# Chunk 1's first channel product as seven half-size products, with a newly searched job order

## The chip, the cores and the metric

The kernel runs on one core of a Trainium2 chip. The core has TensorE (PE in the profile; its weight loads are PEld), VectorE (DVE), ScalarE (ACT), GpSimd (POOL) and SyncE (SP, which here only issues DMAs). TensorE writes its results into eight banks of PSUM, from which VectorE and ScalarE read them. The metric is the time of one execution in microseconds, taken as the median of several runs. A profile is one execution of its own.

## The reference

Two layers follow each other. Shapes: q, k, v are (8 batches, 8 heads, 576 tokens, 64), omega is (128, 64).

```python
def phi(x):                                   # x already scaled by 64 ** -0.25
    h = x @ omega.T - sum(x * x) / 2
    return exp(h - max(h)) / sqrt(128)
q_p, k_p = phi(q), phi(k)
kv  = k_p^T @ v                               # per batch and head, 128 x 64
z   = sum(k_p over tokens)
x   = (q_p @ kv) / (q_p @ z + 1e-6)           # (8, 576, 512) after joining heads

h   = relu(x^T @ w_tok1) @ w_tok2             # over tokens: 576 -> 256 -> 576
u   = x + h^T
out = u + relu(u @ w_ch1) @ w_ch2             # over channels: 512 -> 1536 -> 512
```

The result is float32; the kernel works in float16 with float32 sums in PSUM.

## The kernel before

**Stages.** For each batch b (0 to 7): attention (`attention`), the token mix (`token_mix`, or `token_mix_first` for batch 0), then the channel mix (`channel_mix`) of "chunk" c = b, which covers the batch's first 512 tokens. The last 64 tokens of all batches are gathered and make chunk 8. Of batches 2 to 7, q and k go through DRAM: GpSimd issues DMAs that cast them to float16 into scratch (`load_transposed`, lines 407 to 418), and SP issues DMA transposes that bring them back (line 428, tiles qT and kT). The token mix ends in u, which SP turns with another DMA transpose into uT (line 852), the operand of the channel mix. The first attention jobs of a batch (lines 599 and 707 for k, 669 and 719 for q) read kT and qT.

**Channel mix, two forms.** The first product is u (512 tokens x 512) by w_ch1 (512 x 1536). In the plain form (lines 1178, 1184, 1186) it is 12 jobs, one for each 128 hidden columns: four matmuls of 512 columns into one bank, then one relu by ScalarE or VectorE (line 338 or 340) into tile r3. In the fast form (`channel_in_fast`, matmuls at line 1107) both operands are cut into halves, 2 x 2 blocks, and the four block products are made out of seven, in Winograd's way. It works on three groups of hidden columns (m = 0, 1, 2), each with seven products of four 256-column matmuls into the banks X, Y and Z. It needs four sums of blocks of uT (line 343 through `tt`), eight sums of blocks of w_ch1 (`weight_sums`, made once and kept in one buffer of the qT ring, one of the kT ring and a small tile), three copies per group that keep a bank for later (line 334, into parts of r3, qp and kp buffers), three joins per group (line 1131, VectorE adds a kept copy to a bank) and relus over the joined blocks. The second product has its own seven-product form (`channel_out_fast`, line 989), used by chunks 1 to 8; its sums (tile S) are of 768 columns, and chunk 0 uses the plain form (line 1212).

Which form the first product takes is one number:

```python
if c >= FAST_IN:
    channel_out_fast(c, key, channel_in_fast(c, key, jt))
    return
```

and the sums of the weights are added to the program ahead of that chunk (`if b == FAST_IN: weight_sums(b - 1.0)`).

**The order.** The program builds a list of jobs (1528 of them before), each with its engine, what it depends on and which buffers it takes and gives back. It does not choose their order while building: `ORDER` is a written list of job numbers, found by a search beforehand (negative numbers are filler matmuls that keep TensorE busy in the head, line 1252), `SLOT` says which buffer of a ring each taker gets, and `MOVED` puts single jobs on another engine than their usual one. Each engine works through its own jobs strictly in that order, so a job that waits holds all the jobs of its engine behind it. This goes for SP too, whose queue holds loads back, u transposes and stores in one line, and for GpSimd, which issues the casting DMAs between its sums. Jobs marked `port=True` on VectorE and GpSimd also wait for each other in turn (`turns`).

Of the kernel before, what the change touches and what calls it, by code (L numbers as in the profile page):

```python
# [213 lines left out]
def kernel(  # L214
# [28 lines left out]
    RT = ST // 2  # L243
    RA = R + RT
    NPE = 2
    FAST_IN = 2
    SPLIT = ()
    HALVES = ()
    RW = S * 4 // P
# [1036 lines left out]
```

## Time and profile before

| What | Value |
|---|---|
| Median of 3 runs | 268.33 us (268.24 to 268.38) |
| Profiled execution | 270.67 us |
| Its span, first to last instruction | 268.9 us |
| Granted TensorE clock, mean | 0.998 |
| PE busy | 257.9 us, 96% |
| DVE busy | 231.7 us, 86% |
| ACT busy | 183.0 us, 68% |
| POOL busy | 158.9 us, 59% |

A busy share is an average over the whole span. TensorE's matmuls are pipelined: the mean duration of one (273 ns for 256 columns) is longer than the pitch at which they follow each other, so the cost of a stream is read from the length of an unbroken stretch divided by its count. In a timeline, what stands in brackets at the end of a row is the time that the engine stood idle before it and what ended that.

### The profile page before, as it was taken

Reading aid. Unit: us, or ns where it says so; the run is one execution under the profiler, and the core shown is the slowest. Engines: PE = TensorE matmul, PEld = TensorE weight load, DVE = VectorE, ACT = ScalarE, POOL = GpSimd, SP = SyncE. Lnnn points to the kernel's source line nnn. Section 1 sums busy time; section 2 is a strip of 40 time slices with the busy share of each in tenths; the row PEclk is TensorE's granted clock in tenths of the full one; section 3 lists DMA queues with packets and bytes.
Section 4 is the critical chain, followed back from the end, with each engine's and each line's share of the span. In section 5 each row is a group of like instructions: output and inputs, shape, how many; then the busy total and the mean of one; then the engine's idle time right before and its main releaser. Section 6 shows DMA issues by size and latency. Waiting matters only on the chain.

```text
span 268.9 us, 6989 instructions
## 1 busy us (share of the span) xinstructions
PE 257.9 (96%) x2752; PEld 190.6 (71%) x2752; DVE 231.7 (86%) x494; ACT 183.0 (68%) x425; POOL 158.9 (59%) x160
## 2 busy tenths in 40 slices
PE   4999999999999999989999999999999999999993
PEld 2568455454667985768768777897696788888882
DVE  3999978599999998889999999998987898788982
ACT  1997982089885896879988989878865482273400
POOL 8765553061897966987498852745775004927171
PEclk9999999999999999999999999999999999999999
DMA  7999999999999999999999927844350513040144
GB/s 192 199 208 200 205 207 184 175 220 186 240 168 143 175 207 187 121 198 210 175 222 189 240 85 80 119 85 95 105 152 0 80 67 112 0 157 4 41 146 127
DMA packets 81826, 39.72 MB, mean 148 GB/s; under 512 B 64033, under 2 KB 77729, under 8 KB 81601
## 3 DMA queue, kind: packets, MB, share of 16 engines
q0 software_dynamic: 31712, 17.61, 44.7%
q1 hardware_dynamic: 48560, 19.50, 34.7%
q10 hardware_dynamic: 1520, 2.16, 2.3%
q8 instruction: 21, 0.34, 0.5%
q14 instruction: 13, 0.10, 0.1%
HBM read 35.95 MB, written 16.52 MB: 195 GB/s over the span
## 4 chain that ended last, share of the span: by engine, by line
PE 81%; DMA 7%; POOL 6%; issue 2%; DVE 2%; ACT 1%; POOLq 0%
PE bank L989 23%; PE bank L1107 21%; PE bank L1178 7%; PE bank L1212 4%; PE bank L831 4%; PE bank L844 4%; DMA k<-in_k_dram 4%; DMA uT<-u 3%; PE bank L707 3%; PE bank L796 3%; PE bank L763 2%; PE bank L719 2%; POOL S L343 2%; POOL vs L343 1%; POOL uT L343 1%
## 5 line engine op out<-in xcount | busy, mean ns | idle before, releaser
L562 ACT ACTIVATE kp<-bank 128x512 f16<-128x512 f32 x64 | 35.8, 610 | 13.5 <-PE bank L707 13.1
L338 ACT ACTIVATE r<-bank 128x512 f16<-128x512 f32 (+1 forms) x50 | 29.1, 606 | 20.1 <-PE bank L1107 9.9
L989 PEld LDWEIGHTS <-r 128*128 128x128 f16 x384 | 36.9, 98 | 6.8 <-issue 1.0
L562 ACT ACTIVATE qp<-bank 128x512 f16<-128x512 f32 x64 | 36.7, 631 | 2.5 <-PE bank L719 2.4
L740 DVE TENSOR_REDUCE km<-kp 128x8 f16<-128x1024 f16 x32 | 38.1, 1205 | 0.5 <-ACT kp L562 0.5
L343 POOL TENSOR_TENSOR vs<-v,vs 128x512 f16<-128x512 f16 x22 | 23.7, 1082 | 16.0 <-DVE vs L744 5.5
L1107 PE MATMUL bank<-uT,wc 128*128 128x256 f16 x228 | 30.5, 273 | 1.2 <-DMA uT<-u 1.2
L989 PEld LDWEIGHTS <-S 128*128 128x128 f16 x288 | 27.6, 98 | 4.4 <-POOL S L343 0.2
L1107 PEld LDWEIGHTS <-wc 128*128 128x128 f16 x252 | 23.5, 98 | 5.7 <-DMA uT<-u 1.7
L343 POOL TENSOR_TENSOR S<-r,S 128x768 f16<-128x768 f16 x15 | 24.4, 1641 | 4.5 <-DVE vbd L644 3.4
L989 PE MATMUL bank<-T,r 128*128 128x256 f16 x192 | 23.8, 273 | 0.1
L989 PE MATMUL bank<-T,S 128*128 128x256 f16 x192 | 23.6, 273 | 0.0
L989 PE MATMUL bank<-wc,r 128*128 128x256 f16 x192 | 23.4, 273 | 0.0
L812 ACT ACTIVATE x<-bank,rc 128x64 f16<-128x64 f32 x100 | 22.4, 348 | 0.4 <-DVE rc L803 0.4
L343 POOL TENSOR_TENSOR uT<-uT,uT 128x512 f16<-128x512 f16 x10 | 11.6, 1158 | 17.9 <-PE bank L1107 15.8
L338 ACT ACTIVATE r<-r 128x512 f16<-128x512 f16 (+1 forms) x21 | 16.7, 822 | 7.5 <-DVE r L1131 7.5
L1107 PE MATMUL bank<-uT,qT 128*128 128x256 f16 x126 | 21.7, 272 | 0.0
L847 DVE TENSOR_TENSOR u<-x,bank 128x512 f16<-128x512 f16 x28 | 17.8, 680 | 4.3 <-PE bank L844 4.2
L1107 PE MATMUL bank<-uT,kT 128*128 128x256 f16 x126 | 21.4, 273 | 0.0
L1178 PE MATMUL bank<-uT,wc 128*128 128x512 f16 x88 | 20.5, 380 | 0.0
L969 DVE TENSOR_TENSOR o<-u,bank 128x512 f32<-128x512 f16 x28 | 19.0, 677 | 1.8 <-PE bank L989 1.7
L814 DVE TENSOR_TENSOR x<-bank,rc 128x320 f16<-128x320 f32 x44 | 20.0, 477 | 0.4
(158 smaller groups left out, 612.5 us busy)
## 6 DMA issues: line engine op xcount, KB each, us to landing
out_dram<-o SPq DMA_DIRECT2D x11, 512.0 KB, 4.5
q<-in_q_dram POOLq DMA_DIRECT2D x6, 576.0 KB, 9.2
wc<-in_moe_w_ch_dram POOLq DMA_DIRECT2D x4, 768.0 KB, 13.1
k<-in_k_dram POOLq DMA_DIRECT2D x6, 512.0 KB, 9.4
v<-in_v_dram POOLq DMA_DIRECT2D x6, 512.0 KB, 8.9
out_dram<-o SPq DMA_DIRECT2D x6, 256.0 KB, 3.3
r<-in_q_dram POOLq DMA_DIRECT2D x4, 288.0 KB, 7.6
v<-in_v_dram POOLq DMA_DIRECT2D x4, 256.0 KB, 10.8
```

What stands on the lines that cost most here:

```text
L338: nc.scalar.activation(out=out, in_=in_, func=AF.Relu)
L343: (nc.gpsimd if eng == "POOL" else nc.vector).tensor_tensor(**kw)
L562: nc.scalar.activation(out=out, in_=in_, func=AF.Exp, bias=0.0, scale=1.0)
L740: nc.vector.reduce_max(out=t_km[place("km", (b, hp))], in_=src_, axis=AX.X)
L812: nc.scalar.activation(out=to[:, j], in_=ps[:, j], func=AF.Copy, scale=rc[:, j : j + 1])
L814: nc.vector.tensor_tensor(out=to, in0=ps, in1=rc.unsqueeze(2).broadcast_to((P, NJ + 1, D)), op=ALU.mult)
L831: nc.tensor.matmul(ps, w1m[:, j, tb * P : (tb + 1) * P], x[:, j, :], start=False, stop=(j == NJ - 1))
L847: nc.vector.tensor_tensor(out=t_u[place("u", b)][:, j, :], in0=t_x[place("x", b)][:, j, :], in1=bank(n), op=ALU.add)
L969: nc.vector.tensor_tensor(out=o, in0=a, in1=ps, op=ALU.add)
L989: nc.tensor.matmul(ps[:, j * DH : (j + 1) * DH], a[:, cb, j * P : (j + 1) * P], w[:, cb, :], start=(bank_of(b, j0) not in held and j == j0 ...
L1107: nc.tensor.matmul(ps[:, n, :], w(a)[:, (2 * m + n) * P : (2 * m + n + 1) * P], x_[:, a], start=(what in ("P1", "P2", "P5") and n == 0 and ...
L1178: nc.tensor.matmul(ps, wc1[:, db, cb * P : (cb + 1) * P], moving(db), start=(db == 0), stop=(db == ND - 1))
```

## The change

`FAST_IN` goes from 2 to 1, so chunk 1's first channel product takes the fast form: 12 jobs of four 512-column matmuls are replaced by 21 of four 256-column matmuls, with the block sums, kept copies, joins and relus that belong to them. The sums of the weights are added ahead of chunk 1 and not ahead of chunk 2, with the same eight operations. The list has 1556 jobs. `ORDER`, `SLOT` and `MOVED` are replaced as a whole: the part that loads and transposes batch 0 and works on its attention keeps the order that it has on each engine (but for one filler), and what follows comes from a new search, in which a DMA transpose that is issued late holds the Sync engine. Nothing else of the program differs.

```diff
 ORDER = [
-    2, 38, 16, 3, 7, 6, 4, 9, 12, 10, 0, -8, 41, 1, 14, 39, 42, 40, 47, 48, 8, 11, 13, 21, 22, 19, 17, 5, 78, 49,
...
-    1507, 1520, 1521, 1508, 1509, 1523, 1522, 1516, 1510, 1511, 1525, 1517, 1524,
+    2, 3, 7, 6, 5, 4, 9, 12, 10, 38, 16, 0, 8, 1, -8, 41, 14, 11, 39, 47, 42, 13, 40, 78, 21, 48, 49, 79, 22, 50,
...
+    1545, 1534, 1544, 1535, 1548, 1549,
 ]
 SLOT = (
...
 MOVED = {
...
-    164: "DVE", 167: "DVE", 175: "ACT", 181: "DVE", 185: "DVE", 201: "ACT", 206: "ACT", 208: "DVE", 246: "ACT",
...
+    164: "DVE", 171: "DVE", 173: "DVE", 175: "ACT", 177: "DVE", 181: "DVE", 183: "ACT", 191: "ACT", 196: "ACT",
+    201: "ACT", 202: "ACT", 208: "DVE", 227: "DVE", 244: "DVE", 246: "ACT", 249: "ACT", 261: "DVE", 263: "DVE",
+    278: "DVE", 283: "ACT", 291: "DVE", 303: "POOL", 304: "POOL", 307: "POOL", 308: "POOL", 310: "POOL",
...
 }
@@
     NPE = 2
-    FAST_IN = 2
+    FAST_IN = 1
     SPLIT = ()
```

More of the change, by code (lines that the diff above doesn't have):

```diff
@@ L22 @@
 ORDER = [
[74 rows of a table removed]
[76 rows of a table added]
 ]
 SLOT = (
-    "0001203405067101232540760102330123012460751230021432701142623113003145101237261500434567001253621417"
-    "2150621753341006702115023246105163020133704015231042211507121124306303205126456737421201062402061324"
-    "2201113074125061353027113542131203072261135000431170621452237061221304432567571103611241001041715030"
-    "6221337501163231215013020260321073200100010703124612013205143605627400120546347304507210610110320157"
-    "1420300721233501471320035233112200011221320521731023116120117130614372100420310271260020516724301023"
-    "6725230000411213015637023061102723600532000126030203101200276053120076215110320241567642470362100006"
-    "3007332211237261213236102101614301200111415623037214100571321651720100310110630265310623321775354117"
-    "6203003031213052672420310456017132120231212603105207101053126027754356120701052010202101302113105263"
-    "41010712315012156720400712050333201120117050423160"
+    "0000123405067100112325407601024336027512403012021134270113326230041301512726135100453467002524611337"
+    "5140163100743215074060101212405330202627104331240221317311402157012426315240475667327104061702021200"
+    "4601731201412765022103012301114226315001232220764110521311314200050310001124725610051747415012000376"
+    "1522014751320012301624017511573020643200110120206240320512310576312045123250674102041306354722011113"
+    "2065421720030643700521331020113621050421716021011632312500034262012322670411317603361300542766427173"
+    "5140015163327201031056301410020117361212102413607122031205617320013231406105312467276342113000126710"
+    "3251410023211351042112254323215413031211225076143201150217300453622104510010260023150103306612061347"
+    "0423106351033610241215700614210152312017026502430070532647223005610746537047250171202035223520331320"
+    "065172001243113040352114740312600140312013200165071340"
 )
@@ L111 @@
     103: "DVE", 111: "ACT", 120: "DVE", 137: "DVE", 142: "ACT", 149: "DVE", 151: "DVE", 155: "DVE", 161: "ACT",
-    164: "DVE", 167: "DVE", 175: "ACT", 181: "DVE", 185: "DVE", 201: "ACT", 206: "ACT", 208: "DVE", 246: "ACT",
-    261: "DVE", 269: "ACT", 278: "DVE", 280: "DVE", 291: "DVE", 312: "DVE", 318: "DVE", 324: "DVE", 328: "POOL",
-    330: "POOL", 332: "POOL", 334: "POOL", 349: "ACT", 394: "DVE", 396: "DVE", 402: "ACT", 411: "DVE", 413: "DVE",
-    428: "DVE", 430: "DVE", 433: "ACT", 452: "POOL", 453: "POOL", 455: "POOL", 459: "POOL", 460: "POOL", 478: "ACT",
@@ L116 @@
-    509: "ACT", 510: "ACT", 514: "POOL", 516: "POOL", 517: "POOL", 518: "POOL", 586: "ACT", 595: "DVE", 603: "ACT",
-    617: "ACT", 637: "POOL", 638: "POOL", 639: "POOL", 640: "POOL", 656: "ACT", 690: "POOL", 692: "POOL",
-    694: "POOL", 696: "POOL", 744: "ACT", 778: "ACT", 781: "ACT", 798: "ACT", 813: "POOL", 814: "POOL", 815: "POOL",
-    816: "POOL", 831: "ACT", 832: "ACT", 866: "POOL", 868: "POOL", 869: "POOL", 870: "POOL", 920: "ACT", 940: "ACT",
-    971: "ACT", 992: "POOL", 994: "POOL", 1009: "ACT", 1025: "ACT", 1026: "ACT", 1041: "ACT", 1043: "POOL",
@@ L121 @@
-    1044: "POOL", 1046: "POOL", 1050: "POOL", 1066: "ACT", 1101: "ACT", 1112: "DVE", 1152: "ACT", 1167: "POOL",
-    1168: "POOL", 1169: "POOL", 1170: "POOL", 1174: "DVE", 1185: "ACT", 1186: "ACT", 1202: "ACT", 1217: "ACT",
-    1220: "POOL", 1222: "POOL", 1224: "POOL", 1226: "POOL", 1271: "DVE", 1277: "ACT", 1291: "ACT", 1325: "ACT",
-    1333: "DVE", 1348: "POOL", 1355: "DVE", 1362: "DVE", 1363: "ACT", 1373: "DVE", 1380: "ACT", 1387: "DVE",
-    1395: "ACT", 1396: "ACT", 1397: "POOL", 1398: "POOL", 1400: "POOL", 1404: "POOL", 1426: "POOL", 1427: "POOL",
@@ L126 @@
-    1429: "POOL", 1445: "ACT", 1449: "DVE", 1461: "ACT", 1477: "ACT", 1480: "POOL", 1481: "POOL", 1485: "POOL",
-    1514: "ACT", 1516: "POOL", 1517: "POOL", 1518: "ACT", 1519: "SP", 1520: "ACT", 1521: "SP", 1524: "ACT",
-    1525: "SP",
+    164: "DVE", 171: "DVE", 173: "DVE", 175: "ACT", 177: "DVE", 181: "DVE", 183: "ACT", 191: "ACT", 196: "ACT",
+    201: "ACT", 202: "ACT", 208: "DVE", 227: "DVE", 244: "DVE", 246: "ACT", 249: "ACT", 261: "DVE", 263: "DVE",
+    278: "DVE", 283: "ACT", 291: "DVE", 303: "POOL", 304: "POOL", 307: "POOL", 308: "POOL", 310: "POOL",
@@ new lines @@
+    312: "POOL", 313: "POOL", 314: "POOL", 346: "ACT", 366: "POOL", 368: "POOL", 369: "POOL", 370: "POOL",
+    418: "ACT", 430: "DVE", 472: "ACT", 487: "POOL", 505: "ACT", 506: "ACT", 538: "ACT", 540: "POOL", 542: "POOL",
+    544: "POOL", 546: "POOL", 597: "ACT", 625: "DVE", 628: "ACT", 648: "ACT", 665: "POOL", 666: "POOL", 667: "POOL",
+    668: "POOL", 684: "ACT", 699: "ACT", 716: "ACT", 718: "POOL", 720: "POOL", 724: "POOL", 772: "ACT", 806: "ACT",
+    841: "POOL", 842: "POOL", 843: "POOL", 844: "POOL", 859: "ACT", 876: "ACT", 894: "POOL", 896: "POOL",
@@ new lines @@
+    897: "POOL", 900: "POOL", 979: "DVE", 982: "ACT", 985: "ACT", 1002: "ACT", 1020: "POOL", 1021: "POOL",
+    1037: "ACT", 1053: "ACT", 1054: "ACT", 1069: "ACT", 1070: "ACT", 1074: "POOL", 1077: "POOL", 1078: "POOL",
+    1093: "ACT", 1094: "ACT", 1129: "ACT", 1146: "ACT", 1160: "ACT", 1174: "DVE", 1195: "POOL", 1196: "POOL",
+    1197: "POOL", 1198: "POOL", 1202: "DVE", 1207: "DVE", 1212: "DVE", 1214: "ACT", 1229: "ACT", 1230: "ACT",
+    1234: "DVE", 1246: "ACT", 1248: "POOL", 1249: "POOL", 1252: "POOL", 1254: "POOL", 1269: "ACT", 1270: "ACT",
@@ L129 @@
+    1297: "DVE", 1299: "DVE", 1305: "ACT", 1336: "ACT", 1339: "ACT", 1373: "POOL", 1376: "POOL", 1406: "DVE",
+    1408: "ACT", 1423: "ACT", 1426: "POOL", 1427: "POOL", 1428: "POOL", 1431: "POOL", 1432: "POOL", 1448: "ACT",
+    1449: "ACT", 1455: "POOL", 1461: "DVE", 1466: "DVE", 1472: "ACT", 1488: "ACT", 1496: "DVE", 1505: "ACT",
+    1508: "POOL", 1509: "POOL", 1542: "ACT", 1544: "POOL", 1545: "POOL", 1550: "ACT", 1551: "SP",
 }
```

146 rows, old and new, of the table ORDER are left out of this document.

## The prediction

> **What bounds the kernel now.** I read the page's first part, then a table of engine time by stage, then the chain of waits, then the timelines round the two places where TensorE stands still. In the table the columns behind the window's length are the busy us of PE, weight loads, VectorE, ScalarE and GpSimd, each with its count.
>
> ```profile
> span 268.9 us, 6989 instructions
> PE 257.9 (96%) x2752; PEld 190.6 (71%) x2752; DVE 231.7 (86%) x494; ACT 183.0 (68%) x425; POOL 158.9 (59%) x160
> ...
> 0.00:10.00 10.00, 5.63 (x48) 4.15 (x50) 4.78 (x15) 4.12 (x7) 7.82 (x17) 1.00 0.89 192
> 10.00:20.00 10.00, 9.63 (x183) 5.48 (x178) 9.95 (x24) 10.00 (x27) 7.58 (x11) 1.00 1.21 208
> ...
> 60.00:70.00 10.00, 10.00 (x86) 5.02 (x85) 8.97 (x21) 9.37 (x19) 3.44 (x4) 1.00 0.99 195
> 70.00:80.00 10.00, 10.00 (x106) 5.90 (x103) 9.54 (x26) 8.22 (x23) 9.98 (x11) 1.00 1.15 203
> 80.00:90.00 10.00, 10.00 (x117) 8.01 (x115) 9.72 (x18) 6.75 (x15) 8.28 (x7) 1.00 1.22 141
> 90.00:100.00 10.00, 10.00 (x137) 9.13 (x134) 9.46 (x27) 9.30 (x29) 8.37 (x11) 1.00 1.10 206
> 100.00:110.00 10.00, 9.30 (x86) 5.61 (x84) 8.18 (x18) 6.80 (x14) 6.71 (x8) 1.00 1.46 182
> 110.00:120.00 10.00, 8.67 (x109) 6.94 (x109) 8.72 (x16) 8.41 (x23) 8.81 (x8) 1.00 1.07 141
> ```
>
> The 11.0 us without a matmul (268.9 - 257.9) lie in three places: 4.74 in the first 20 us (20 - 5.63 - 9.63), 2.03 between 100 and 120 (0.70 + 1.33), and the rest, some 4.2, behind the last matmul. Every other window from 20 to 260 has PE at 10.00. So a TensorE microsecond saved behind the head is saved from the end, as long as nobody else makes TensorE wait. VectorE at 9.5 of 10 from 70 on is the engine that could. The granted clock is 1.00 in these windows.
>
> **Term 1: fewer matmul columns.** Chunk 1's first product was 12 jobs of four 512-column matmuls (48). It becomes three groups of seven products, each four matmuls of 256 columns (84). The pitch of both kinds stands in the chain; the second row below is one of chunks 2 to 8, which already run exactly this code.
>
> ```profile
> 72.09 1.73 PE bank L1178 x8
> 160.64 2.18 PE bank L1107 x20
> ...
> L1107 PEld LDWEIGHTS <-wc 128*128 128x128 f16 x252 | 23.5, 98 | 5.7 <-DMA uT<-u 1.7 <-issue 1.2
> L884 PEld LDWEIGHTS <-r 128*128 128x128 f16 x8 | 1.0, 139 | 0.0
> ```
>
> 1.73 / 8 = 0.216 us and 2.18 / 20 = 0.109 us: removed 48 x 0.216 = 10.36, added 84 x 0.109 = 9.17, together **-1.19 us**. Bound: the added 84 need 84 weight loads instead of 48; at 98 ns they fit under the 109 of the matmul. The slowest load of any row is 139 ns; at that pitch 84 x 0.139 = 11.7 and the change costs 1.3. I take 109, as the row is the same line with the same shapes.
>
> The Trainium skill (TensorE: Matmul & The Clock Gate, Back-to-back issue gap) gives N / 2.4 + 2.5 ns for an isolated warm stream, which is 216 and 109 ns here, but also says that in a real stream of load and matmul pairs the spacing at 512 columns is about 131 ns. By that the removed jobs are worth only 48 x 0.131 = 6.3 us, as an estimate from that page, and the change would lose time on TensorE. The trace speaks for the first rule and against the second (216 ns).
>
> **Term 2: more work beside it.** Counting the jobs of both lists by kind and engine, at the means of these rows:
>
> ```profile
> L1131 DVE TENSOR_TENSOR r<-r,bank 128x512 f16<-128x512 f32 x21 | 14.0, 678 | 1.6 <-PE bank L1107 1.3 <-ACT r L334 0.2
> L340 DVE TENSOR_SCALAR r<-bank 128x512 f16<-128x512 f32 x11 | 7.4, 678 | 2.4 <-PE bank L831 1.8 <-PE bank L1178 0.4
> L340 DVE TENSOR_SCALAR r<-r 128x1024 f16<-128x1024 f16 x12 | 5.2, 459 | 0.1
> L340 DVE TENSOR_SCALAR r<-r 128x512 f16<-128x512 f16 x9 | 2.5, 282 | 0.6 <-POOL r L343 0.5
> L343 DVE TENSOR_TENSOR S<-S,r 128x768 f16<-128x768 f16 x14 | 7.7, 553 | 0.2
> L343 DVE TENSOR_TENSOR uT<-uT 128x512 f16<-128x512 f16 x5 | 2.0, 418 | 0.0
> L334 DVE CAST kvsb<-bank 128x130 f16<-128x130 f32 x9 | 2.5, 293 | 2.0 <-PE bank L772 1.8
> L338 ACT ACTIVATE r<-bank 128x512 f16<-128x512 f32 x48 | 28.3, 616 | 19.8 <-PE bank L1107 9.9 <-PE bank L831 8.6 <-PE bank L1178 1.0
> L334 ACT COPY kp<-bank 128x512 f32<-128x512 f32 x21 | 11.7, 596 | 5.9 <-PE bank L1107 5.8
> L343 POOL TENSOR_TENSOR uT<-uT,uT 128x512 f16<-128x512 f16 x10 | 11.6, 1158 | 17.9 <-PE bank L1107 15.8
> L343 POOL TENSOR_TENSOR S<-r,S 128x768 f16<-128x768 f16 x15 | 24.4, 1641 | 4.5 <-DVE vbd L644 3.4 <-DVE S L343 0.6 <-DVE r L340 0.5
> ```
>
> VectorE: nine joins and a kept copy more (10 x 0.68), two sums of 768 (1.1), three of 512 (1.25), five relus from SBUF or a bank (2 x 0.46, 2 x 0.28, 0.68); less three relus of a bank (2.0), two weight sums (1.1), and one each of a kv copy, an out copy and a token relu (0.29 + 2 x 0.68). Net **+6.5**, so 238 of about 266 us. ScalarE: eight kept copies more (4.8), nine relus from a bank less (5.5), seven others moved to it (some 4.4): about +3.6 of its 86 idle us, and five stores more to issue, late in its queue. GpSimd: three sums of 512 for chunk 1 and two weight sums more, two sums of each size less: +1.2. None of it is on TensorE, so its price there is zero while it keeps ahead. What hides it: the 37 us that VectorE idles now, of which 2.3 lie between 60 and 100, the neighbourhood of the new product. Without cover it costs up to 6.5 - 2.3 = 4.2. A gain is excluded, it is only added work; I take 0.2.
>
> VectorE and GpSimd also take turns by written waits on a shared port, and behind a waiting VectorE instruction stands all its queue, bank reads included. In the trace VectorE has waited this long for GpSimd sums:
>
> ```profile
> DVE vbd L644 <- POOL r L343: 1.1, 1, 1.1
> DVE r L340 <- POOL r L343: 0.5, 1, 0.5
> ```
>
> That is 1.6 us, over more than the 25 GpSimd sums of the two last rows above: at most 0.06 each. The three of chunk 1 and two weight sums make 0.3 of VectorE time, at worst 3 x 1.16 + 2 x 1.64 = 6.8; the row of what was suffered is the nearer one, and 0.3 hides in the idle time like the rest.
>
> **Term 3: the order.** Engine by engine the new list agrees with the old in TensorE's first 48 entries (but for one filler matmul that changes places with a product), VectorE's first 46, ScalarE's 33 and GpSimd's 27, so the head's 4.74 us stay. Behind it both stalls are DMA transposes on the SP queue:
>
> ```profile
> 101.37 0.29 PE L599 MATMUL bank<-omT,kT 64*128 64x128 f16 x4 [0.70 <-DMA kT<-k]
> 117.41 0.61 PE L1107 MATMUL bank<-uT,wc 128*128 128x256 f16 x4 [1.21 <-DMA uT<-u]
> ...
> 82.13 4.07 SPq L852 DMA_TRANSPOSE uT<-u  x1
> 86.30 3.85 SPq L428 DMA_TRANSPOSE qT<-q  x1
> 90.33 3.34 SPq L428 DMA_TRANSPOSE kT<-k  x1
> ...
> 108.60 4.15 SPq L852 DMA_TRANSPOSE uT<-u  x1
> ...
> DMA to landing us min/median/max: 4.4/5.6/8.8
> ```
>
> Each transpose holds SP for 2 to 4 us and the next one queues behind it: chunk 2's u, then batch 4's q, then its k, which came 0.70 late. Chunk 3's u landed 8.8 us after its issue (108.60 to 117.4), 1.21 late. Adding up the pitches of the TensorE jobs listed between the last token product of a chunk and the first use of its transposed u, I get, for chunks 1 to 7, 8.4, 9.9, 8.6, 9.3, 10.3, 9.5, 9.3 us before and 8.7, 11.1, 9.7, 11.6, 9.7, 11.4, 9.7 after. Chunk 3 needed 8.6 + 1.21 = 9.8 and gets 9.7. Batch 4's first k product stands 21.0 us behind chunk 2's token product, was 19.6: 1.4 more against 0.70 late. SP's order round both is the same. So both stalls should go, but for 0.1: **-1.8**. Bounds: -1.91, or 0 if the landings move with the order.
>
> What comes late next? Chunks 3, 5 and 7 at 9.7 are 0.1 short if their transposes land as slowly as 8.8, and have 3 us to spare at the median 5.6. Batch 2's first k product is wanted 1.7 us earlier (51.1 to 49.4 of TensorE work). Its tail cast moves up in GpSimd's queue past a weight sum and chunk values of batch 1, which VectorE now makes, so it can issue before the 40.13 of now. The third early use is the second half of the first channel weights, which chunk 0 now takes one job earlier:
>
> ```profile
> 18.62 0.80 POOL L473 DMA_DIRECT2D wc<-in_moe_w_ch_dram  x1 [0.43 <-DMA w<-in_moe_w_tok_dram]
> ...
> 30.31 0.52 POOL L407 DMA_DIRECT2D q<-in_q_dram  x1 [2.50 <-DMA wc<-in_moe_w_ch_dram]
> ...
> 27.72 2.76 PE L1178 MATMUL bank<-uT,wc 128*128 128x512 f16 x12
> ```
>
> It lands at 30.3, when GpSimd's waiting DMA is let go. The new order has two query products more ahead of chunk 0 (2 x 0.22) and then 0.86 + 0.22 + 0.55 + 0.86 before the use, so 27.72 + 0.44 + 2.49 = 30.65: free by 0.3. For these and for lateness that I can't see I add **+0.3**; bounds 0 and the 2.03 that the old order suffered, and the value is nearer the low end because the old one suffered it in only two places of seven chunks.
>
> The end: the last matmul group is still six 256-column matmuls, one read and small stores; VectorE has one sum of chunk 8 more and GpSimd one less, between products. I take 0, within 0.3.
>
> **The sum.** The profiled execution took 270.67 us, 268.9 of it span; the median of the plain runs, 268.33, lies 0.57 under the span. The differences apply to either: -1.19 + 0.2 - 1.8 + 0.3 = -2.5. Predicted **265.8 us** (span about 266.4).
>
> **Rivals.**
> *The stalls only move* (batch 2's k at 49.4, or a u that lands in 8.8 again): one of them goes (0.7), the other comes back. 268.33 - 1.19 - 0.7 + 0.5 = 266.9, the 0.5 being Term 2's 0.2 and the 0.3. For it: the landings of 4.4 to 8.8 us depend on what else moves. Against: the margin of every u but chunk 5's is wider than it was, and chunk 5's is 0.1 short of the slowest need.
> *All of it is eaten*: stalls of 3 us in new places, 268.3, no change. Half the lists are new, yet the old list had only 2.03 us of such waits behind the head.
> *VectorE becomes the bound* between 60 and 100. Its place is the joins of chunk 1, which free TensorE's accumulators; it decides once the windows there pass 9.9 of 10. Price 4.2 of surplus, less the 1.19, less the 1.9 us of stalls that a delayed TensorE no longer feels: +1.1, so 269.4. For it: 9.46 to 9.72 now. Against: the list hands two weight sums to GpSimd, and chunk 2 runs the same joins in the 90 to 100 window with TensorE at 10.00.
> *Weight loads set the pitch*: +1.3 in place of -1.19: 268.33 + 1.3 - 1.8 + 0.5 = 268.3, or 269.6 if the stalls stay and the 0.5 doesn't come. The 98 ns row speaks against it. The skill's spacing of pairs, above, would be of this kind, and the 216 ns row denies it.
>
> **How the numbers follow.** Forecast 0.52 (own range 264.9 to 266.6), moved stalls 0.22, all eaten 0.10, VectorE 0.13, weight loads 0.03. A measurement here tells 0.2%, 0.54 us, from no change. Faster is the first two, 0.74; within 0.2% the third and a little, 0.12; slower 0.14. The range 264.8 (both stalls gone, tail 0.3 better) to 268.2 takes in the first two and part of the third; VectorE's case is left out.
>
> **What would show it.** Term 1: 84 matmuls more at line 1107 with 0.109 pitch and none at 1178 beyond chunk 0. Term 3: no wait of TensorE for uT or kT over 0.3 us; PE at 10.00 in all windows from 20 to 258. Term 2: VectorE near 238 us busy, and TensorE idle put down to joins under 0.3. It is wrong if PE idles more than 1.5 us between 20 us and its last matmul, or if VectorE's windows round 60 to 100 read 9.9 with TensorE below 10.

## The result and the profile after

The changed kernel takes **276.47 us** (median of four runs, 275.84 to 277.1) against 268.36 before (268.24 to 268.86): ratio **1.0299** with a 95% interval of 1.0272 to 1.0326. It is slower by 8.1 us, where 2.5 us of gain were forecast; the forecast's range ended at 268.2. The profiled execution took 275.84 us with a span of 274.1, 5.2 more than the profiled span before.

The page's first part, and the table of engine time by stage (columns as in the prediction: busy us of PE, weight loads, VectorE, ScalarE and GpSimd, then the granted clock; the last two are the share of the DMA engines and GB/s). All lines of code stand two further down than before.

```profile
span 274.1 us, 7086 instructions
PE 260.5 (95%) x2788; PEld 195.7 (71%) x2788; DVE 242.5 (88%) x506; ACT 186.3 (68%) x431; POOL 159.9 (58%) x161
```

```profile
40.00:50.00 10.00, 6.54 (x70) 3.79 (x67) 9.21 (x14) 2.38 (x8) 4.94 (x5) 0.86 1.36 178
47.00:51.00 4.00, 4.00 (x25) 1.97 (x24) 2.93 (x9) 1.79 (x7) 0.00 (x0) 0.57 1.27 142
50.00:60.00 10.00, 9.89 (x74) 4.76 (x72) 7.02 (x16) 2.49 (x8) 0.00 (x0) 0.97 0.54 107
60.00:70.00 10.00, 9.51 (x99) 5.15 (x99) 8.87 (x17) 9.55 (x22) 7.73 (x9) 1.00 0.98 141
80.00:90.00 10.00, 9.98 (x94) 6.54 (x92) 10.00 (x18) 6.99 (x18) 8.40 (x9) 1.00 1.23 194
100.00:110.00 10.00, 10.00 (x116) 8.24 (x114) 9.49 (x22) 9.41 (x25) 9.30 (x12) 1.00 1.12 209
110.00:120.00 10.00, 10.00 (x92) 6.52 (x89) 9.86 (x19) 8.66 (x19) 7.31 (x5) 1.00 1.30 159
```

From 100 to 120, where the two waits of before stood, TensorE now reads 10.00. Most of the loss is in one place: from 40 to 50 it stands still for 3.46 us, and from 47 to 51 its mean clock is 0.57, which costs 4 x 0.43 = 1.7 us more. Before, this window read 10.00 at clock 1.00:

```profile
40.00:50.00 10.00, 10.00 (x86) 5.13 (x82) 6.72 (x20) 2.71 (x9) 2.77 (x4) 1.00 1.29 179
```

The timeline of the place after the change (start, length, engine, line, operation, tiles, in square brackets the idle time before it and its releaser):

```profile
37.82 0.51 DVE L345 TENSOR_TENSOR kT<-wc 128x768 f16<-128x768 f16 x1
...
38.48 1.63 POOL L345 TENSOR_TENSOR qT<-wc 128x768 f16<-128x768 f16 x1 [0.81 <-DVE vs L746]
38.48 2.78 DVE L345 TENSOR_TENSOR vs<-v,vs 128x512 f16<-128x512 f16 x2
...
41.38 1.65 POOL L345 TENSOR_TENSOR qT<-wc 128x768 f16<-128x768 f16 x1
42.39 3.73 DVE L345 TENSOR_TENSOR vs<-v,vs 128x512 f16<-128x512 f16 x1
42.95 0.94 POOL L387 DMA_DIRECT2D v<-in_v_dram  x1
43.91 1.65 POOL L345 TENSOR_TENSOR qT<-qT,wc 128x768 f16<-128x768 f16 x1
46.17 0.40 PE L765 MATMUL bank<-vs,kp 128*128 128x65 f16 x8 [3.46 <-DVE vs L345]
```

TensorE waits for `vs`, one of batch 1's four value products (each value times a factor of its token and head), and that VectorE instruction took 3.73 us. The group of these products tells what it should take; the first row is of the kernel before, the second of the changed one:

```profile
L343 DVE TENSOR_TENSOR vs<-v,vs 128x512 f16<-128x512 f16 x10 | 6.5, 680 | 0.2 <-DMA v<-in_v_dram 0.2
```

```profile
L345 DVE TENSOR_TENSOR vs<-v,vs 128x512 f16<-128x512 f16 x10 | 11.2, 1140 | 0.1
```

Ten instructions of one shape in both, 680 ns each before and 1140 after. They are not all of the same batches: of batch 1's four, VectorE makes all now and made two before. The pair at 38.48 took 2.78 us for 2 x 0.68 and the next 3.73; both lie beside GpSimd's weight sums (tile qT, 1.65 us each), and the long one begins beside one sum and ends 0.56 after the next (43.91 + 1.65 = 45.56). Before, the first weight sum on GpSimd was let go at 56, after 13.41 us of waiting:

```profile
56.18 1.63 POOL L343 TENSOR_TENSOR kT<-wc 128x768 f16<-128x768 f16 x1 [13.41 <-DVE qT L343]
```

In the written list the first four of GpSimd's five weight sums stand behind all of batch 1's value products. But GpSimd is a queue of its own and runs ahead of the list unless something holds it. What should hold it is the written turn, and a turn waits for the last VectorE job **that itself takes turns**. Batch 1's value products take none (`port=b >= 2`), so GpSimd waited only for a VectorE weight sum, which began at 37.82 (the row at 38.48 names the small VectorE instruction just behind it), and ran at 38.48 what the list has behind all four products and behind batch 1's u adds.

### The profile page after: what moved, and what is told of

It reads as the page before. It is cut to its first block, busy times and chain, and to the rows that moved or that the text cites. A ratio compares the mean times of both kernels' runs of the same rounds, so it can differ in the third digit from the quotient of the medians.

```text
span 274.1 us, 7086 instructions
## 1 busy us (share of the span) xinstructions
PE 260.5 (95%) x2788; PEld 195.7 (71%) x2788; DVE 242.5 (88%) x506; ACT 186.3 (68%) x431; POOL 159.9 (58%) x161
## 4 chain that ended last, share of the span: by engine, by line
PE 85%; DVE 6%; ACT 5%; issue 1%; POOL 1%; DVEq 0%; POOLq 0%; ACTq 0%
PE bank L991 27%; PE bank L1109 27%; PE bank L833 5%; PE bank L846 5%; PE bank L1214 3%; PE bank L709 3%; PE bank L798 3%; DVE vs L345 2%; PE bank L721 2%; PE bank L765 2%; ACT qp L564 2%; DVE km L742 2%; PE bank L520 1%; ACT kp L564 1%; DVE r L342 1%
## 5 line engine op out<-in xcount | busy, mean ns | idle before, releaser
L340 ACT ACTIVATE r<-bank 128x512 f16<-128x512 f32 (+1 forms) x44 | 25.5, 619 | 20.6 <-PE bank L1180 8.2
L1109 PE MATMUL bank<-uT,wc 128*128 128x256 f16 x264 | 36.0, 273 | 0.0
L1109 PEld LDWEIGHTS <-wc 128*128 128x128 f16 x288 | 27.2, 98 | 4.1 <-issue 0.5
L345 POOL TENSOR_TENSOR S<-r,S 128x768 f16<-128x768 f16 x14 | 22.9, 1639 | 7.6 <-DVE vbd L646 4.9
L814 ACT ACTIVATE x<-bank,rc 128x64 f16<-128x64 f32 x100 | 23.1, 347 | 3.7 <-DVE rc L805 3.7
L1109 PE MATMUL bank<-uT,qT 128*128 128x256 f16 x144 | 25.1, 273 | 0.0
L1109 PE MATMUL bank<-uT,kT 128*128 128x256 f16 x144 | 25.1, 273 | 0.0
L340 ACT ACTIVATE r<-r 128x512 f16<-128x512 f16 (+1 forms) x23 | 18.3, 835 | 7.4 <-DVE r L1133 7.1
L345 POOL TENSOR_TENSOR S<-S,r 128x768 f16<-128x768 f16 x6 | 9.8, 1639 | 22.2 <-DVE S L345 9.7
L345 POOL TENSOR_TENSOR uT<-uT 128x512 f16<-128x512 f16 x10 | 11.6, 1157 | 11.0 <-DMA uT<-u 9.3
```

Source lines behind the costliest of these rows:

```text
L340: nc.scalar.activation(out=out, in_=in_, func=AF.Relu)
L345: (nc.gpsimd if eng == "POOL" else nc.vector).tensor_tensor(**kw)
L814: nc.scalar.activation(out=to[:, j], in_=ps[:, j], func=AF.Copy, scale=rc[:, j : j + 1])
L1109: nc.tensor.matmul(ps[:, n, :], w(a)[:, (2 * m + n) * P : (2 * m + n + 1) * P], x_[:, a], start=(what in ("P1", "P2", "P5") and n == 0 and ...
```

## The experiments

Theory: VectorE instructions with two inputs in SBUF and GpSimd's sums shut each other out, the change brought them together where no turn keeps them apart, and the half clock follows from TensorE's wait. Rivals: VectorE simply has too much work; the new list wants batch 2's keys too early; the first product itself costs more than counted.

**The changed kernel once more.** No edit.

> The changed kernel once more, as the reference of this chip: 276.5 us, TensorE idle some 4.4 us between 20 and 70 us, one stall of 3.5 us at 42.7 us that ends with a VectorE product into the tile vs.

275.49 us (275.2 to 277.49), 1.0252 (1.017 to 1.0334). The profile shows the same wait, 3.4 us, for the same product. The loss belongs to the kernel, not to one execution.

**Turns for batch 1's value products.**

```diff
-  give=[("v", b)], port=b >= 2)
+  give=[("v", b)], port=b >= 1)
```

> One word is changed: batch 1's products into vs take turns with GpSimd too (port from batch 1 on, not from batch 2 on); no engine gets more or less work. Contention theory (the product that ran 3.73 us in place of 0.68 was held by GpSimd's weight sums): all products of batch 1 at 0.68 us, the first GpSimd weight sum starts behind the last of them, the 3.5 us stall is below 0.5, the clock in 40 to 50 us is 1.00 and the time falls by 7 to 10 us, to 266 to 269. Overload theory (VectorE simply has too much to do between 30 and 46 us): the queue of VectorE is as long as before less at most 0.5 us, the stall stays above 2.5 us, time above 274.

275.04 us (274.82 to 276.88), 1.0232 (1.0168 to 1.0297), no clear gain on the repeated run. Timeline, VectorE, GpSimd and TensorE:

```profile
41.09 0.68 DVE L345 TENSOR_TENSOR vs<-v,vs 128x512 f16<-128x512 f16 x1
44.41 4.79 DVE L498 TENSOR_TENSOR T<-wc 128x1536 f16<-128x1536 f16 x1
...
44.19 1.65 POOL L345 TENSOR_TENSOR qT<-wc 128x768 f16<-128x768 f16 x1
46.73 1.65 POOL L345 TENSOR_TENSOR qT<-qT,wc 128x768 f16<-128x768 f16 x1
...
49.65 0.38 PE L798 MATMUL bank<-kvsb,qp 128*128 128x65 f16 x4 [3.15 <-DVE x L816]
```

The value product is back at 0.68. GpSimd's sums come some 3 us later and fall on the next VectorE instruction with two SBUF inputs and no turn: a sum for the second product's weights (T), 4.79 us where it took 0.95 elsewhere. The bank reads queue behind it, and TensorE waits 3.15. The mechanism held and the forecast of time did not: the hold moved on by one instruction.

**Four of GpSimd's five weight sums on VectorE.** The fifth (job 310) comes later in the list and stays.

```diff
-    278: "DVE", 283: "ACT", 291: "DVE", 303: "POOL", 304: "POOL", 307: "POOL", 308: "POOL", 310: "POOL",
+    278: "DVE", 283: "ACT", 291: "DVE", 310: "POOL",
```

> The four weight sums that GpSimd makes go to VectorE at the same place of the list (four times 0.55 us more on VectorE, four times 1.64 less on GpSimd). Contention theory: nothing runs on GpSimd's port beside batch 1's products, which take 0.68; stall below 0.5 us, clock 1.00, time 266 to 270, the 2.2 us of added VectorE work being placed behind the stall. Overload theory: VectorE has still more to do, so the stall is no shorter than 2.5 us and the time stays at 276 or goes above.

277.09 us (276.12 to 278.95), 1.0302 (1.0231 to 1.0372). Nothing is held any more, TensorE reads 10.00 from 40 to 50, and a new wait takes the place of the old one. Timeline, GpSimd, SP's queue, TensorE:

```profile
43.29 0.86 POOL L420 DMA_DIRECT2D k<-in_k_dram  x1 [1.08 <-DMA k<-in_k_dram]
...
47.42 0.53 POOL L409 DMA_DIRECT2D q<-in_q_dram  x1
...
47.53 9.10 SPq L430 DMA_TRANSPOSE kT<-k  x1
...
59.05 0.61 PE L709 MATMUL bank<-omT,kT 64*128 64x128 f16 x8 [5.10 <-DMA kT<-k]
```

With the sums gone, GpSimd reaches batch 3's casts at 43.29 instead of 62, and batch 2's key transpose, issued at 47.53, holds SP for 9.10 us (3.17 before the change, 3.71 in the changed kernel). Batch 2's first k product was wanted at 53.95 and had to wait.

**Filler matmuls ahead of the product that waits.** Fourteen matmuls of zeros into an idle bank, which add work and change no output.

```diff
-    ... 284, 245, 228, 182, ...
+    ... 284, 245, -2, -2, -2, -2, -2, -2, -2, -2, -2, -2, -2, -2, -2, -2, 228, 182, ...
```

> Fourteen filler matmuls of 512 columns (3.0 us at 0.216) are put right ahead of the matmul group that stalls, so TensorE works while it would wait; the held products stay as they are. If the halved clock behind the stall comes from TensorE standing idle: clock in 40 to 60 us at 1.00, the 512-column matmuls behind the stall at 0.216 and not at 0.43, time 3 to 4.5 us lower, 272 to 273.5, and the wait before the group some 0.5 us. If the slow matmuls have another cause: time within 1 us of 276.5 and the matmuls behind still slow.

274.22 us (274.04 to 274.59), 1.0188 (1.0135 to 1.0242). The clock stays at 1.00 from 40 to 60, and TensorE's idle time at the place falls to 0.75:

```profile
46.37 0.40 PE L765 MATMUL bank<-vs,kp 128*128 128x65 f16 x8 [0.75 <-DVE vs L345]
```

So the half clock does come from TensorE's standing still. Without it the kernel wins 1.3 us against the repeated run beside it, less than the 3 to 4.5 expected and near the 1.7 read from the window; the value product is as late as it was.

**Turns for the T sums too.**

```diff
-  deps=[*j_wc2, *j_T[-1:]]))
+  deps=[*j_wc2, *j_T[-1:]], port=True))
-  give=[("v", b)], port=b >= 2)
+  give=[("v", b)], port=b >= 1)
```

> The four products of batch 1's chunk values and the four sums that prepare the second channel weights (T, 0.95 us each) all take written turns with GpSimd's weight sums, so no VectorE operation with two SBUF inputs can overlap them. Shared port as the whole cause: T at 0.95 each, no TensorE wait over 0.7 us between 40 and 70, clock 0.99 or more there, the 4.4 us of idle time and 3.8 us of half-clock matmuls gone: 266 to 268 us. Late transpose (rival: the list itself wants batch 2's keys too early): TensorE waits 1 us or more at the first k product of batch 2 for the DMA of kT, clock below 0.9 behind it: 270 to 275 us. GpSimd's sums, now behind T, push the loads of batch 2's values back to about 50 us, which the port theory takes to be early enough (they are used near 57).

271.24 us (270.82 to 272.13), 1.0069 (1.0024 to 1.0114): 4 to 5 us better than the changed kernel but not the 266 to 268 expected, and TensorE stands at 10.00 and clock 1.00 from 40 to 50. The transpose rival fails here: batch 2's first k product comes at 55.04 with no wait for a DMA. One thing that is left are late values. GpSimd issues their load between its sums, at 53.91, and a product of batch 2 waits for it:

```profile
53.91 0.94 POOL L387 DMA_DIRECT2D v<-in_v_dram  x1
...
60.82 0.69 DVE L345 TENSOR_TENSOR vs<-v,vs 128x512 f16<-128x512 f16 x1 [0.64 <-DMA v<-in_v_dram]
...
62.81 0.22 PE L772 MATMUL bank<-vbd,kpt 128*128 128x130 f16 x1 [0.30 <-POOL vbd L345]
64.90 0.30 PE L798 MATMUL bank<-kvsb,qp 128*128 128x65 f16 x4 [0.61 <-ACT kvsb L336]
```

**Batch 3's casts behind batch 2's value product.** On top of the four sums on VectorE.

```diff
-    ... 306, 308, 564, 565, 300, ... 206, 563, 401, 447, 207, ...
+    ... 306, 308, 300, ... 206, 401, 447, 564, 565, 563, 207, ...
```

> The four weight sums on VectorE, as in the run before, and batch 3's three casts on GpSimd set behind batch 2's chunk value product, so that they do not run beside batch 2's transposes. If the casts made the key transpose hold SP for 9.1 us: it holds 3 to 4 us, lands before 53.9, the 5.1 us wait at batch 2's first k product goes, PE at 9.9 or more from 40 to 70 at clock 1.00: 266 to 268 us. If the transpose is late for another reason (its own place in SP's queue, batch 2's own casts): the hold stays near 9 and the wait above 4, 275 to 277 us.

Four executions took 277.72 to 284.3 us, too far apart for a ratio. What can be read early in its timeline is the transpose, SP's queue first, then TensorE (lines of code stand four higher in this list):

```profile
47.68 3.67 SPq L426 DMA_TRANSPOSE kT<-k  x1
...
80.78 0.40 PE L705 MATMUL bank<-omT,kT 64*128 64x128 f16 x8 [3.41 <-DMA kT<-k]
...
95.69 0.61 PE L717 MATMUL bank<-qT,omT 64*128 64x512 f16 x2 [6.01 <-DMA qT<-q]
```

With the casts out of the way the transpose holds SP for 3.67 us and the 5.1 us wait is gone: the casts beside it were its cause. But they now issue at 63.6, and batch 3's transposes are late in their turn. The sizes of those later waits come from a single profile; only that they are there is used.

**The loads ahead of the sums.** As the kernel with both turns, and batch 2's two value loads before GpSimd's weight sums.

```diff
-    ... 390, 303, 393, 307, 394, 304, ...
+    ... 390, 393, 394, 303, 307, 304, ...
```

> As the first kernel of this call, and batch 2's two value loads ahead of GpSimd's weight sums instead of between them. Shared port: the same 266 to 268 us, and if the first kernel lost time to late values this one is faster by that. If loads issued while VectorE works matter themselves (descriptors written by GpSimd over the same port): the loads near 41 us stretch VectorE's products to above 0.8 us. Late transpose: the wait for kT at batch 2's first k product stays as in the first kernel.

270.51 us (269.79 to 271.04, ten runs), 1.0031 (1.0005 to 1.0058). Page and windows of this kernel:

```profile
span 267.9 us, 7086 instructions
PE 258.5 (96%) x2788; PEld 194.9 (73%) x2788; DVE 238.3 (89%) x506; ACT 186.4 (70%) x431; POOL 159.9 (60%) x161
```

```profile
40.00:50.00 10.00, 10.00 (x103) 5.54 (x102) 9.29 (x24) 3.52 (x13) 1.79 (x3) 1.00 1.32 181
50.00:60.00 10.00, 9.72 (x87) 4.77 (x86) 7.73 (x15) 6.35 (x13) 9.29 (x9) 1.00 0.95 164
60.00:70.00 10.00, 9.68 (x110) 7.12 (x109) 8.73 (x19) 9.13 (x19) 7.76 (x7) 1.00 1.05 181
```

No wait of TensorE over 0.32 us behind the head, clock 1.00: **6.0 us of the 8.1 are back**, from two turns and two loads moved. The two medians come from different chips; by the ratios to the kernel before on each chip (1.0252 and 1.0299 against 1.0031 and 1.0077) it is 4.7 to 7.2. VectorE's busy time falls from 242.5 to 238.3; the 4.2 between them were instructions that stood waiting and were booked as busy (the ten value products alone fall from 11.2 to 6.7). The same kernel once more, beside the joined one below:

> The same kernel without the joins, unchanged, beside it on the same chip: 258.5 us of TensorE busy time, 1.003 of the time before, between 1.000 and 1.006.

270.5 us, 1.0077 (1.0045 to 1.0108), TensorE busy 258.3. It is no faster than the kernel before, where 2.5 us of gain were forecast for a changed kernel without disturbance. The runs of the kernel before, and the joined one, further down, look into that rest.

**Two of the four value products back on GpSimd.**

```diff
-    164: "DVE", ... 208: "DVE", 227: "DVE", 244: "DVE", 246: "ACT",
+    164: "DVE", ... 208: "DVE", 246: "ACT",
```

> Two of batch 1's four chunk value products go back from VectorE to GpSimd, as before the change (1.08 us there, 0.68 on VectorE); nothing else is changed, no turns are added. Port theory: GpSimd's queue then holds its weight sums back by itself until these products are done near 43, so the two products left on VectorE run in 0.7 to 1.1, and what is hit next is the second T sum (0.95 to 3 or more): TensorE waits 1 to 4 us between 44 and 55, 271 to 276 us. If the loss came from VectorE's added work rather than from the overlap, taking 1.4 us from it gives at most 1.4 us back: 275.

270.93 us (270.03 to 271.64), 1.006 (1.0029 to 1.0091), below what the port theory expected, and far below the 275 of the work theory. Timeline, GpSimd and VectorE:

```profile
36.84 2.75 POOL L345 TENSOR_TENSOR vs<-v,vs 128x512 f16<-128x512 f16 x2 [1.57 <-PE bank L1180]
...
44.47 1.52 DVE L498 TENSOR_TENSOR T<-wc 128x1536 f16<-128x1536 f16 x1
```

Two products in GpSimd's own queue hold its sums back by themselves. One T sum is still stretched, from 0.95 to 1.52, but TensorE does not wait for it. 1.4 us less VectorE work gave back 4.6 to 5.5 us (against 275.49 and 276.47): it was the overlap and not the work.

**The kernel before, profiled once more.** No edit.

> The kernel before, unchanged, profiled once more. The prediction took 1.8 us from the two waits for DMA transposes (0.70 and 1.21) that its one profiled execution showed. If they are part of every execution: both stand again near 101 and 117, the span is 268 to 269. If that execution was a late one (its span lies 0.6 above the median time of the plain runs): one or both are missing, TensorE reads 10.00 from 20 to 260, the span is 266.4 to 267.5, and the 1.8 us were never there to be won against the median.

```profile
span 268.2 us, 6989 instructions
PE 258.5 (96%) x2752; PEld 191.4 (71%) x2752; DVE 232.0 (87%) x494; ACT 182.8 (68%) x425; POOL 158.8 (59%) x160
...
100.00:110.00 10.00, 10.00 (x95) 6.49 (x93) 9.76 (x20) 7.40 (x17) 7.70 (x8) 1.00 1.43 166
...
114.39 1.47 PE L989 MATMUL bank<-T,r 128*128 128x256 f16 x12 [1.32 <-DVE o L969]
```

The wait for keys at 101 is missing, and the wait near 115 is put down to VectorE instead of a transpose: 1.32 us in all against 2.03 in the first profile. One of the two waits is gone and the other has a new place and releaser: what they add up to is not a fixed part of the old kernel.

**The kernel before with twelve more cuts.** A job is exchanged with its neighbour at twelve places, one of them shown, so that runs of matmuls on half the rows are cut in two.

```diff
-    ... 437, 550, 556, 438, 440, ...
+    ... 437, 550, 438, 556, 440, ...
```

> The kernel before with twelve of TensorE's jobs in its list exchanged with a neighbour, so that a run of matmuls on half the rows (64 of 128: the products of k and q with omega, and the token tail) is cut in two at twelve more places, 104 changes between the two kinds in place of 80; the work is the same. Changed list cuts finer (the theory for what is left when the port is free): each cut costs the 0.10 us of entering and the 0.11 of leaving that the trace shows around such runs, 12 x 0.21 = 2.5 us of TensorE busy time, and the time is 2 to 3 us longer. If the order of the jobs costs TensorE nothing, busy time stays within 0.3 us of 257.9 and the time is the same within 0.5 us.

273.82 us (273.2 to 274.49), 1.0139 (1.005 to 1.0228).

```profile
PE 262.0 (96%) x2752; PEld 190.9 (70%) x2752; DVE 233.3 (86%) x494; ACT 183.0 (67%) x425; POOL 159.2 (58%) x160
```

TensorE is busy 262.0 us with the same matmuls, 3.5 to 4.1 more than in the two profiles of the kernel before (258.5 and 257.9): about 0.3 us for each cut, more than the 2.5 us expected for all and clear of the 0.3 allowed for no cost. Every job keeps its buffer.

**Casts gated.** The sums on VectorE, and batch 3's casts made to depend on batch 1's u adds in the list.

```diff
-            load_transposed(b, b + key_of("lt", b))
+            load_transposed(b, b + key_of("lt", b), gate if b == 3 else ())
+        if b == 1:
+            gate = uT[0].deps
```

> The four weight sums on VectorE, and batch 3's casts made to wait for the u adds of batch 1 (near 54), between the two runs in which they issued at 43 (batch 2's transposes late) and at 63 (batch 3's late). If the casts' place alone made both waits: no TensorE wait over 0.7 us from 40 to 100, the key transpose of batch 2 holds SP 3 to 4 us, 269.5 to 271 us, as with the turns. If the sums on VectorE cost time of their own: VectorE reads above 9.9 in a window where TensorE is below 9.9, above 271 us.

276.74 us (276.52 to 277.11), 1.0256 (1.0182 to 1.033).

```profile
43.48 0.86 POOL L420 DMA_DIRECT2D k<-in_k_dram  x1 [1.07 <-DMA k<-in_k_dram]
...
59.16 0.61 PE L709 MATMUL bank<-omT,kT 64*128 64x128 f16 x8 [4.70 <-DMA kT<-k]
```

The edit does not do what it says: such a dependence orders the written list and puts no wait into the program where no data passes, so the casts issued at 43.48 again. It counts as a repeat of the run with the sums on VectorE (277.09), and a middle place of the casts stays untried.

**Five runs joined.** The fastest form of the change, with one or two TensorE jobs of other kinds moved past a run of half-row matmuls at five places, one of them shown.

```diff
-    ... 565, 300, 422, 395, 439, 423, 424, 200, 205, 396, ...
+    ... 565, 300, 200, 205, 422, 395, 439, 423, 424, 396, ...
```

> The changed kernel with the turns and the two loads first (the fastest of its forms so far, TensorE busy 258.5, 1.003 of the time before), and five runs of half-row matmuls joined with their neighbours by moving one or two TensorE jobs of other kinds past them, 80 changes between the kinds in place of 90. If the finer cutting is what is left: TensorE busy falls by 5 x 0.21 to 5 x 0.29 = 1.0 to 1.5 to some 257.2, and the time by as much, 1.0 us or more under the same kernel without the joins, level with the kernel before or up to 0.3% under it. If what is left is of another kind (later reads, the end): busy time as it was, no difference over 0.4 us. A move that makes a product late shows as a new wait of TensorE and gives the gain back.

278.97 us (277.84 to 280.84), 1.0395 (1.0343 to 1.0447). Timeline and windows:

```profile
57.49 0.49 PE L705 MATMUL bank<-omT,kT 64*128 64x128 f16 x8 [0.28 <-ACT kp L560]
59.50 0.37 PE L717 MATMUL bank<-qT,omT 64*128 64x512 f16 x1 [0.86 <-ACT o L332]
...
56.00:58.00 2.00, 1.30 (x29) 0.88 (x26) 0.53 (x1) 1.65 (x4) 2.00 (x3) 1.00 1.12 213
58.00:60.00 2.00, 0.75 (x8) 0.32 (x8) 1.96 (x3) 2.00 (x6) 1.42 (x3) 1.00 0.78 57
60.00:62.00 2.00, 1.76 (x5) 0.48 (x5) 1.54 (x6) 2.00 (x5) 0.37 (x1) 0.63 1.00 104
62.00:64.00 2.00, 2.00 (x7) 0.34 (x5) 0.00 (x0) 1.58 (x4) 1.70 (x2) 0.52 1.31 255
```

The jobs that were moved away had been the work of TensorE while ScalarE read the products' banks. Joined, the products wait for ScalarE again and again (4.5 us of TensorE idle time behind 20 us, 0.9 without the joins), and the clock halves here too. TensorE's busy time is 262.4, where 257.2 was expected; the half clock makes some 1.7 of the 4.1 more, and the rest lies in the rows of the q and k products (lines 705, 717 and 667), whose matmuls stand apart between the waits: 29.6 us for all three, 26.7 without the joins. The cuts cost, by the run with twelve more, but these five were buying something dearer, and this run says nothing on the price of a cut. So the theory that the rest could be won by joining fell.

## Why the prediction was wrong, point by point

**The step that failed** is Term 2's paragraph on turns. It priced GpSimd's sums "at most 0.06 each", from the waits that VectorE had suffered before, and took 0 of them. The sums behind those waits take turns, which kept them away from VectorE; the waits were no price of an overlap without a turn. It then took for granted that VectorE and GpSimd always take turns. The code says for each job whether it does, and batch 1's value products and the T sums do not. Term 3 even named that batch 1's values are now made by VectorE, but read it only as room in GpSimd's queue. The price measured: 3.46 us of wait and 1.7 of half clock; with the turns in place and two loads moved the median fell by 6.0.

The Trainium skill (SBUF — State Buffer, Who interferes with whom) states that a VectorE instruction with two inputs in SBUF and a GpSimd instruction that reads SBUF exclude each other for whole instructions, and that the order of issue decides which one blocks. This case agrees that they hold each other up: 0.68 became 3.73, and 0.95 became 4.79. The prediction left the rule out.

**Term 1** was right in its pitch and short by an item. A chunk 1 stretch of the changed kernel in its chain of waits:

```profile
73.11 2.29 PE bank L1109 x20
```

That is 20 x 0.109 and 0.11 more at its head, behind two q products. Behind any run of half-row matmuls the first matmul comes 0.1 late, and so does the run itself; by the run with twelve more cuts each costs 0.3. Counted from the order of the matmuls behind the first 28 us, the old list has 29 such runs and the new one 33. Four more at 0.2 (the two 0.1 of the rows) to 0.3 are 0.8 to 1.2 us, most or all of the 1.19 that the columns save. TensorE's busy time in the undisturbed form is 258.3 to 258.5, where Term 1 gave 257.9 - 1.19 = 256.7. Behind the first 20 us, where nothing of the head counts, it is 242.9 in both profiles of this form, and 242.6 and 242.8 in the two of the kernel before: the saving is gone whole. That the four runs took it is a sum and not an experiment. The Trainium skill (TensorEngine Tiling (Array Packing), Key Properties) says that a change of tiling mode drains TensorE, which would be of this kind; the 0.3 us is from these runs.

**Term 2's work** was right: VectorE 238.3 in the undisturbed form against 238 forecast, and no wait for the joins. In the changed kernel VectorE reads 10.00 from 80 to 90 with TensorE at 9.98, so the rival in which VectorE is the bound was close there and cost 0.02.

**Term 3** got its events right and their worth wrong. Both waits are gone from 100 to 120. But the 1.8 us came off the median, and the second profile of before shows that the waits change from execution to execution. In every execution of the kernel before whose span is on record, the time is 1.7 to 1.8 us above the span. So the median of 268.33 is a span of about 266.5, and the profiled execution (270.67, span 268.9) was a long one; the prediction set this span beside that median as if both were one execution. The two profiles less their waits are 268.9 - 2.03 = 266.9 and 268.2 - 1.32 = 266.9. An execution near the median thus held little or nothing of these waits, and there was little to win. This is argued from the times; no trace of such an execution exists. *The stalls only move*, the rival with the most weight, came true in the runs with the sums on VectorE (5.10 and 4.70 for batch 2's keys), not in the changed kernel itself.

**The whole:** 276.5 is 10.7 above 265.8. The overlap and its half clock are 6.0, by the run that takes them away. TensorE's busy time is 1.7 above Term 1. Between 20 and 70 the undisturbed form idles 0.95 (0.35, 0.28 and 0.32), 0.65 more than the 0.3 for lateness. Some 2.3 us remain, and up to 1.8 of them are Term 3's, if the median held nothing of the two waits. That split is argued and not shown: the timed runs of this form have a median span 0.8 above its profiled one, and no trace shows why. What the prediction named as showing it wrong, more than 1.5 us of TensorE idle time behind 20 us, was there: 4.4.

## What to carry to other kernels

When an order lets two engines share something only by written turns, list which instructions take turns and which do not, and ask of every newly placed one what it can now run beside: an in-order queue runs ahead of the list until something holds it. Price an overlap from an overlapped instruction, not from the waits of a kernel that avoids it. Take a saving off the execution in which it was read: a median may not hold the wait that one profile shows. When one engine's wait is removed, look at what that engine does earlier: here the casts, freed by 19 us, made a transpose late and cost as much as was won.

## What the runs showed of the hardware

A VectorE instruction held by GpSimd does not always use the gap between two sums: the 3.73 us product had 0.88 us free (43.03 to 43.91, while GpSimd issued a load) and needs 0.68. Issuing a load alone does not hold it: in the gated run a product at 41.60 took 0.68 beside the same load at 41.47. With two products back on GpSimd, a T sum did use such a gap, in which a load was issued as well: it ran from 44.47 to 45.99, and GpSimd's sums ended at 45.16 and began again at 46.05. Why the one gap was used and the other not stays open.

Round its longer waits here TensorE runs at half clock for about 3.4 us or twice that. After 3.46 us idle, 4 us read 0.57, which is 4 x 0.43 x 2 = 3.4 us at half. With turns for the values alone, beside a wait of 3.15, 6 us read 0.50, and the windows on either side (48 to 49 and 55 to 57) 0.84 and 0.87, together 6.8; here it began before the wait had ended:

```profile
49.00:55.00 6.00, 5.35 (x18) 1.83 (x18) 4.38 (x13) 1.13 (x5) 0.00 (x0) 0.50 1.23 205
```

In the joined run no single wait passed 0.86 us, and the clock still read 0.63 and 0.52 from 60 to 64, after 1.95 us of idle time in pieces between 56 and 60 (0.70 and 1.25 in the two windows above). From 88 to 92 of the same run, 1.43 us of idle time in pieces left the clock at 1.00. The Trainium skill (TensorE: Matmul & The Clock Gate, Part 1: The HAM clock gate) gives a free-running activity window of about 3.4 us; the lengths agree, while the joined run shows that short waits in a row can be enough.

Batch 2's key transpose held SP for 9.10 and 8.97 us in the two runs with batch 3's casts issued just ahead of and beside it, and for 2.00 to 4.33 us in the others. It is the same transfer each time, so what runs beside a transpose changes how long it holds the queue here.
